# Batch 1's v product behind its scores, x of pair 2 two products behind its v product, and three k transposes moved from TensorE to DMA

## The chip, the cores and the metric

The kernel runs on one core of one Trainium2 chip. The metric is the device time of one execution in microseconds (us), the median of several runs. A ratio in this text is the mean time of one kernel's runs over the mean of the other's runs of the same rounds; it is not quite the ratio of the quoted medians.

Engine names in the profile: PE is TensorE (matrix products), PEld its weight loads, DVE is VectorE, ACT is ScalarE, POOL is GpSimd, SP is SyncE. `banks` is the kernel's name for the buffers in PSUM that TensorE writes. "L583" is line 583 of the kernel's file; the changed kernel has 16 or so more lines, so the same code there has another number.

## The reference

Attention with projected keys and values (Linformer), then a feed-forward layer with a three-way maximum:

```python
batch, n_heads, seq, head_dim = 8, 8, 1024, 64; k_proj = 64
k_proj = einsum('ks,bhsd->bhkd', E, k);  v_proj = einsum('ks,bhsd->bhkd', F, v)
attn   = softmax(q @ k_proj^T / sqrt(64)) @ v_proj
x      = attn.transpose(0, 2, 1, 3).reshape(8192, 512)
out    = maximum(maximum(x @ w1, x @ w2), x @ w3) @ w_out     # d_ff = 768
```

## The kernel before

The feed-forward products of batch b fill TensorE, 512 columns at a time. The attention work of batch b+1 is placed between them, in "visits": a plan says after which step of the feed-forward which piece stands. `(1, 2)` is the visit after step 2 of the second half of the batch; `(1, (3, "mid"))` is inside step 3, after two of its three products of four matmuls. `kproj`, `vproj` are the projections of k and v, `kt` turns the projected k on TensorE, `sc` computes the scores of a pair of heads and their exponentials, `za` the sums and values of a pair (`values` reads the projected v, called vp), `qd` packs q and turns it by DMA into qT, `ld` loads a batch.

```python
    def kt(b):                       # k of batch b turned on TensorE
        def f():
            t, ns = two()
            t = t.bitcast(BF16)[:, 0]
            for gg in range(2):
                nc.tensor.transpose(
                    out=t[:, gg * P:(gg + 1) * P], in_=kps[b][:, gg, :], identity=ident
                )
            pe(0.2)
            kpTs[b] = att.tile([P, NPAIR, KP], BF16, name="kpT")
            copy("v", kpTs[b].rearrange("a (y x) k -> a x y k", x=2),
                 t[:, 0:2 * P].rearrange("a (x y k) -> a x y k", x=2, y=2), ns, 0.3)
        return f

    def plan(b):
        n = b + 1
        if b == 0:
            c1 = (SPC, SPC)
            return {
                ...
                (0, 7): [qd(1, 2), za(0, 2, *c1)],       # q of batch 1 turned, in two DMAs
                (0, 8): [za(0, 3, *c1)],
                (1, 0): [kproj(1)],
                (1, 1): [kt(1)],
                (1, 2): [vproj(1), ld(2)],
                (1, (3, "mid")): [sc(1, 0, now=True), sc(1, 1)],
                (1, 4): [za(1, 0), sc(1, 2, now=True)],
                ...
        # b = 3, 4, 5:
            out[1, 2] = [kproj(n + 1), vproj(n + 1)] + out[1, 2]
            out[1, 3] = [kt(n + 1)]                      # then ld(n + 2)
            out[1, 6] += [sc(n + 1, 0)]
    ...
                up_first({                               # the very first product
                    ...
                    (0, 1, 3): [lambda: v_pair(2), lambda: x(2)],
                    (0, 1, 5): [lambda: v_pair(3), ld(1)],
```

`x(g)` is the values of pair g (which read what `v_pair(g)` and a DVE copy made) and the scaling by the softmax sums. All loads are cast by DMA from GpSimd's queue, in order; SyncE's queue issues qT's transposes, the stores and a few small transfers, also in order.

The softmax here doesn't subtract the row's maximum and nothing guards it: scores larger than these inputs give would overflow.

## Time and profile before

403.06 us (402.93 to 403.52 in 3 runs).

| what | reading | from |
|---|---|---|
| PE busy | 388.4 of 400.4 us | the page, part 1 |
| products of 128x512 | start 216 ns apart | the timeline of PE |
| DMA engines | 9 tenths busy up to 80 us | the page, part 2 |
| longest PE waits after the start | 1.04 us for batch 1's v, 0.45 us for vp of pair 2 | waits and timeline |

Parts 1 and 2 of the page of the kernel before: busy us of each engine with its share of the span, then tenths in 40 slices of 10 us.

```profile
PE 388.4 (97%) x2244; PEld 176.7 (44%) x2286; DVE 203.5 (51%) x319; ACT 151.0 (38%) x242; POOL 34.2 (9%) x49
...
PE   7999989999999999999999999999999999999996
...
PEclk9999999999999999999999999999999999999999
DMA  9999999968799998999989959990890229020202
```

PE is the bound engine nearly everywhere, at its full clock, and DMA is about full through the first eight slices (80 us). PE's busy share alone would not prove that it is at its peak, because pipelined matmuls overlap in the record. The spacing of starts does: 216 ns for 512 columns. The Trainium skill ("TensorE: Matmul & The Clock Gate", section "Wait — 56ns, not 53.3ns?") gives 215.7 ns for warm back-to-back matmuls of that size, and this trace agrees.

The list of waits of PE in the kernel before: who waited for whom, us in total, how often, the longest. A wait of 1.5 us of the warm-up stands above these lines and is left out.

```profile
...
PE banks L346 <- DMA v_t<-in_v_dram: 1.0, 1, 1.0
PE banks L490 <- DMA k_t<-in_k_dram: 0.9, 1, 0.9
PE banks L687 <- issue: 0.8, 5, 0.2
...
PE banks L232 <- DVE vp L102: 0.7, 2, 0.5
PE banks L583 <- DVE xT L309: 0.3, 2, 0.2
PE banks L212 <- DVE m L652: 0.3, 1, 0.3
```

L346 is the projection of k or v, L490 the first k product of batch 0, L232 sums and values, L212 scores, L583 the three up products, L687 the down product. A wait "for issue" here sits where one matmul record is missing from the trace. The line of L346 is the largest wait that a new order of work could take away. The timeline of PE around it, kernel before: start us, duration us, engine, line, what, count, and in brackets the idle time just before and what ended it.

```profile
45.76 2.75 PE L583 MATMUL banks<-xT,w_sb 128*128 128x512 bf16 x12
48.44 1.06 PE L346 MATMUL banks<-k_t,efT 128*64 128x256 bf16 x16
...
52.04 0.27 PE L432 MATMUL banks<-ident,kp 128*128 128x128 bf16 x2
52.15 2.75 PE L583 MATMUL banks<-xT,w_sb 128*128 128x512 bf16 x12
55.95 1.06 PE L346 MATMUL banks<-v_t,efT 128*64 128x256 bf16 x16 [1.04 <-DMA v_t<-in_v_dram]
56.94 1.90 PE L583 MATMUL banks<-xT,w_sb 128*128 128x512 bf16 x8
58.77 0.63 PE L212 MATMUL banks<-qT,kpT 64*64 64x512 bf16 x8
59.33 1.04 PE L583 MATMUL banks<-xT,w_sb 128*128 128x512 bf16 x3
```

The v product starts at 55.95, the moment its load has landed (issued at 25.64, landed at 55.90), and the scores follow at 58.77. The scores read qT. The trace's record of the issue of qT's first half, at 43.95 us in the kernel before, says when it landed:

```profile
DMA to landing us min/median/max: 13.2/13.2/13.2
```

That is at 57.16, so at 58.77 nobody waits for it.

The timeline of PE around pair 2's values (L232 at 21.25), kernel before:

```profile
19.31 1.04 PE L583 MATMUL banks<-xT,w_sb 128*128 128x512 bf16 x4
20.19 0.61 PE L516 MATMUL banks<-v_t,efT 128*128 128x128 bf16 x8
21.25 0.30 PE L232 MATMUL banks<-pT,vp 64*64 64x256 bf16 x4 [0.45 <-DVE vp L102]
21.48 0.60 PE L583 MATMUL banks<-xT,w_sb 128*128 128x512 bf16 x2
```

And around the turn of batch 5's k (L432):

```profile
206.82 0.28 PE L432 MATMUL banks<-ident,kp 128*128 128x128 bf16 x2
206.93 1.24 PE L583 MATMUL banks<-xT,w_sb 128*128 128x512 bf16 x5
```

The record of the two transposes lasts 0.28 us, but the next product starts 0.11 us after the first of them: that, and not the duration, is what they cost a pipelined PE.

### The profile page before, as it was taken

To read this page: it belongs to the slowest core of one execution; us is meant where nothing else is said; L and a number is where in the kernel's file an instruction comes from. 1 tells how busy PE (TensorE), PEld (TensorE's weight loads), DVE (VectorE), ACT (ScalarE), POOL (GpSimd) and SP (SyncE) were. 2 spreads that over 40 slices of the span, in tenths; PEclk is the share of its full clock that TensorE was granted. 3 is DMA by queue.
4 is the path that set the end of the run, shared out by engine and by line. 5 is a ranking of instruction groups with operands and counts; after the bars stand their busy time and mean duration, and the time that the engine had idled before them with its cause. 6 is when DMAs were issued, how large, how long until landed. Compare 5 with 4: busy or idle time off the path is not lost.

```text
span 400.4 us, 5708 instructions
## 1 busy us (share of the span) xinstructions
PE 388.4 (97%) x2244; PEld 176.7 (44%) x2286; DVE 203.5 (51%) x319; ACT 151.0 (38%) x242; POOL 34.2 (9%) x49
## 2 busy tenths in 40 slices
PE   7999989999999999999999999999999999999996
PEld 3444443353444445444454445444454444444443
DVE  2348746762683525736274544744267342745251
ACT  2535428527222462253323532245323533132312
POOL 7440002000400200010020000100000000000000
PEclk9999999999999999999999999999999999999999
DMA  9999999968799998999989959990890229020202
GB/s 159 205 206 208 230 204 156 235 137 156 203 187 198 221 218 193 223 183 209 224 221 178 236 133 269 178 242 26 204 217 5 103 67 252 0 105 2 105 0 105
DMA packets 66330, 66.09 MB, mean 165 GB/s; under 512 B 30624, under 2 KB 58784, under 8 KB 66304
## 3 DMA queue, kind: packets, MB, share of 16 engines
q0 software_dynamic: 29104, 30.41, 47.0%
q1 hardware_dynamic: 37056, 35.20, 34.3%
q8 instruction: 17, 0.28, 0.3%
q10 hardware_dynamic: 144, 0.13, 0.1%
q14 instruction: 9, 0.07, 0.1%
HBM read 69.73 MB, written 16.97 MB: 217 GB/s over the span
## 4 chain that ended last, share of the span: by engine, by line
PE 84%; DMA 9%; DVE 2%; issue 2%; ACT 1%; POOL 0%; DVEq 0%; ACTq 0%; POOLq 0%
PE banks L583 56%; PE banks L687 18%; DMA v_t<-in_v_dram 8%; PE banks L346 3%; PE banks L232 2%; PE banks L212 2%; DMA k_t<-in_k_dram 2%; DVE xT L309 1%; PE banks L257 1%; ACT zi_all L298 1%; ACT zl L292 1%; PE banks L490 1%; DVE m L652 0%; PE banks L461 0%; PE banks L516 0%
## 5 line engine op out<-in xcount | busy, mean ns | idle before, releaser
L583 PE MATMUL banks<-xT,w_sb 128*128 128x512 bf16 x1119 | 254.8, 379 | 2.6 <-issue 0.8
L583 PEld LDWEIGHTS <-w_sb 128*128 128x128 bf16 x1152 | 109.9, 98 | 136.1 <-issue 8.5
L652 DVE TENSOR_TENSOR m<-banks,h1s 128x512 f32<-128x512 f32 x90 | 62.1, 690 | 135.3 <-ACT h1s L648 92.7
L648 ACT COPY h1s<-banks 128x512 f32<-128x512 f32 x90 | 52.6, 585 | 120.3 <-PE banks L583 118.8
L687 PE MATMUL banks<-wout_sb,hT 128*128 128x512 bf16 x370 | 85.6, 379 | 1.0 <-issue 0.8
L593 DVE TENSOR_TENSOR hT<-banks,m 128x512 bf16<-128x512 f32 x90 | 62.3, 692 | 9.3
L687 PEld LDWEIGHTS <-hT 128*128 128x128 bf16 x378 | 35.2, 98 | 47.4 <-issue 5.6
L102 ACT COPY o_sb<-banks 128x512 f32<-128x512 f32 (+1 forms) x56 | 32.6, 582 | 57.9 <-PE banks L687 57.6
L223 ACT ACTIVATE pT<-banks 128x1024 bf16<-128x1024 f32 (+1 forms) x36 | 32.8, 932 | 18.1 <-PE banks L212 18.1
L309 DVE TENSOR_TENSOR xT<-banks,zi_all 128x1024 bf16<-128x1024 f32 x28 | 33.1, 1219 | 11.7 <-PE banks L232 6.9
L201 POOL DMA_DIRECT2D q_t<-in_q_dram x7 | 6.1, 878 | 193.8 <-DMA qT<-q_p 118.8
L346 PEld LDWEIGHTS <-efT 128*64 128x64 bf16 x224 | 11.6, 110 | 4.5 <-issue 3.0
L102 DVE CAST vp<-banks 64x256 bf16<-64x256 f32 (+1 forms) x18 | 7.1, 397 | 12.5 <-ACT vp L102 9.5
L102 ACT CAST vp<-banks 64x256 bf16<-64x256 f32 x14 | 5.1, 364 | 21.4 <-PE banks L346 21.3
L232 PE MATMUL banks<-pT,vp 64*64 64x512 bf16 (+1 forms) x144 | 11.4, 364 | 0.7 <-DVE vp L102 0.7
L212 PE MATMUL banks<-qT,kpT 64*64 64x512 bf16 (+1 forms) x144 | 11.4, 362 | 0.4 <-DVE m L652 0.3
L292 ACT ACTIVATE zl<-banks 128x512 f32<-128x512 f32 (+1 forms) x12 | 8.9, 739 | 6.3 <-PE banks L232 5.3
L102 DVE COPY q_p<-q_t 128x1024 bf16<-128x1024 bf16 x28 | 10.4, 435 | 0.5 <-DMA q_t<-in_q_dram 0.5
L346 PE MATMUL banks<-v_t,efT 128*64 128x256 bf16 x112 | 7.3, 273 | 1.0 <-DMA v_t<-in_v_dram 1.0
L102 DVE COPY o_sb<-banks 128x512 f32<-128x512 f32 (+1 forms) x9 | 5.8, 653 | 4.5 <-PE banks L667 4.5
L346 PE MATMUL banks<-k_t,efT 128*64 128x256 bf16 x112 | 7.4, 276 | 0.0
L461 PE MATMUL banks<-warm_f 128*128 128x512 f32 x8 | 6.0, 895 | 1.5 <-DVE warm_f L175 1.5
(63 smaller groups left out, 120.9 us busy)
## 6 DMA issues: line engine op xcount, KB each, us to landing
out_dram<-o_sb SPq DMA_DIRECT2D x30, 512.0 KB, 4.6
zi_all<-zd SPq DMA_DIRECT2D x20, 512.0 KB, 8.0
q_t<-in_q_dram POOLq DMA_DIRECT2D x7, 1024.0 KB, 10.1
k_t<-in_k_dram POOLq DMA_DIRECT2D x7, 1024.0 KB, 16.4
v_t<-in_v_dram POOLq DMA_DIRECT2D x7, 1024.0 KB, 21.9
zi_all<-zd POOLq DMA_DIRECT2D x4, 512.0 KB, 7.6
w_sb<-in_moe_w_dram POOLq DMA_DIRECT2D x4, 384.0 KB, 11.1
k_t<-in_k_dram POOLq DMA_DIRECT2D x2, 512.0 KB, 8.7
```

The lines of the kernel that those rows point to most:

```text
L102: done = {"v": nc.vector.tensor_copy, "s": nc.scalar.copy, "g": nc.gpsimd.tensor_copy}[eng](out=o, in_=i)
L212: nc.tensor.matmul(out=t[c * HALF:(c + 1) * HALF, hp, 0:n * P], lhsT=kpTs[b][rows, g, :], rhs=qTs[b][rows, at:at + n, :], start=True, stop ...
L223: nc.scalar.activation(out=pTs[b, g, lo], in_=t, func=AF.Exp, scale=scale)
L232: nc.tensor.matmul(out=t[hp * HALF:(hp + 1) * HALF, c, 0:nsi * HALF], lhsT=w(rows, hp), rhs=p[rows, hp, :], start=True, stop=True,)
L292: nc.scalar.activation(out=zl, in_=t, func=AF.Ln)
L309: nc.vector.tensor_tensor(out=xTs[b][:, g, lo:lo + nsi, :].rearrange("a (c s) p -> a c (s p)", c=2), in0=t, in1=zi, op=ALU.mult,)
L346: nc.tensor.matmul(out=t[hh * HALF:(hh + 1) * HALF, 0:width], lhsT=efT[:, si, (kv - 1) * KP:kv * KP], rhs=qkv[b][kv][:, heads[hh], si, :], ...
L583: nc.tensor.matmul(out=h, lhsT=w_sb[i][:, ct, jt * P:(jt + 1) * P], rhs=xTs[b][:, ct, ch * SPC:(ch + 1) * SPC, :], start=(ct == first), st ...
L593: nc.vector.tensor_tensor(out=o, in0=h, in1=other, op=ALU.max)
L648: nc.scalar.copy(out=h1s, in_=h[0][0])
L652: nc.vector.tensor_tensor(out=m12, in0=h[1][0], in1=h1s, op=ALU.max)
L687: nc.tensor.matmul(out=o_ps, lhsT=hTs[b, ch][:, jt, tt * P:(tt + 1) * P], rhs=wout_sb[:, jt, :], start=(jt == 0), stop=(jt == NJT - 1),)
```

## The change

Three parts. A: batch 1's v product goes behind its scores, so that it does not wait for its load, and its k product and turn go one step later. B: pair 2's v product goes two products earlier, so that the copy of vp runs behind products. C: k of batches 5 to 7 is turned by a DMA on SyncE's queue instead of TensorE and a DVE copy; the next batch's loads wait for that DMA.

```diff
+            if i == 0 and b - 1 in turned:          # in load(): q waits for the turned k
+                after(dma, turned[b - 1])
+    def k_pair(b, g):
+        if b in turned:
+            return kpTs[b][:, g % 2, (g // 2) * KP:(g // 2 + 1) * KP]
+        return kpTs[b][:, g, :]
 ...
-                    lhsT=kpTs[b][rows, g, :],
+                    lhsT=k_pair(b, g)[rows],
 ...
+    def kd(b):
+        def f():
+            kpTs[b] = att.tile([P, 2, 2 * KP], BF16, name="kpT2")
+            turned[b] = nc.sync.dma_start_transpose(
+                out=kpTs[b], in_=kps[b].rearrange("a g x -> a (g x)")
+            )
+        return f
 ...
-                (1, 0): [kproj(1)],
-                (1, 1): [kt(1)],
-                (1, 2): [vproj(1), ld(2)],
-                (1, (3, "mid")): [sc(1, 0, now=True), sc(1, 1)],
+                (1, 1): [kproj(1)],
+                (1, 2): [kt(1)],
+                (1, (3, "mid")): [sc(1, 0, now=True), sc(1, 1), vproj(1), ld(2)],
 ...
-            out[1, 2] = [kproj(n + 1), vproj(n + 1)] + out[1, 2]
-            out[1, 3] = [kt(n + 1)]
+            out[1, 2] = [kproj(n + 1), kd(n + 1), vproj(n + 1)] + out[1, 2]
 ...
-                    (0, 1, 3): [lambda: v_pair(2), lambda: x(2)],
+                    (0, 1, 1): [lambda: v_pair(2)],
+                    (0, 1, 3): [lambda: x(2)],
```

More of the change, by code (lines that the diff above doesn't have):

```diff
@@ L203, in load @@
                 after(dma, last_T[b - 1])
+            if i == 0 and b - 1 in turned:
[4 more added lines that the diff above has]
+        return kpTs[b][:, g, :]
+    turned = {}
     def scores(b, g, lo, nsi):
@@ L758, in plan @@
             out[0, 4] = [qd(n + 1)]
-            out[1, 2] = [kproj(n + 1), vproj(n + 1)] + out[1, 2]
-            out[1, 3] = [kt(n + 1)]
+            out[1, 2] = [kproj(n + 1), kd(n + 1), vproj(n + 1)] + out[1, 2]
             out[1, 6] += [sc(n + 1, 0)]
         if n + 2 < B:
-            out[1, 3] += [ld(n + 2)]
+            out[1, 3] = [ld(n + 2)]
         return out
```

## The prediction

> **What bounds the kernel now.** TensorE. The busy table gives PE 388.4 of 400.4 us. In the timeline 128x512 products start 216 ns apart almost everywhere, at a granted clock of 1.0; the Trainium skill ("TensorE: Matmul & The Clock Gate", section "Wait — 56ns, not 53.3ns?") gives 215.7 ns for warm back-to-back matmuls, and the trace agrees. From batch 2 on the list of waits has no PE wait on another engine of 0.1 us or more. So idle time can be won only before about 77 us; elsewhere only PE work removed counts.
>
> **The change, costed.**
>
> A. Batch 1, 48 to 60 us. The list of waits has one PE wait of 1.04 us for batch 1's v, which lands at 55.90 (timeline: v product at 55.95). After, the v product (0.99 us) stands behind the scores, so v is there. But the scores come early: from 45.76 to 58.77 is 13.0 us; without the v product (1.1 with its switch) and the wait (1.1) they are due at about 56.5. They read qT of pairs 0 and 1, whose DMA transpose was issued at 43.95 and landed at 57.16. The DMA engines are 9 tenths busy up to there, so this landing should not move. I expect a new PE wait of about 0.7 us on qT before batch 1's first scores. One switch between products (0.09 us) goes. Gain about 0.45 us, not 1.1.
>
> B. Pair 2. Before, the values waited 0.45 us for the copy of vp (v product at 20.19, copy 20.90 to 21.20, values 21.25). The v product now stands two products (0.43 us) earlier, but its slice of v landed only at 20.05. It starts at about 20.1 after waiting 0.3 us, and the values still come 1.06 us later, near 21.15. Gain about 0.1 us, and the wait for qT in A, bound by DMA, swallows most of it.
>
> C. k of batches 5 to 7 turned by DMA. Removes six PE transposes, 0.055 us each start to start: 0.11 us per batch, 0.33 us in all, on the saturated PE; also three DVE copies of 0.28 us, off the path. (The skill, same page, "Part 4: PE-mode transpose", says about 275 ns each in a kernel; this trace shows 55.) The DMA transposes are two blocks each against qT's 32; behind two output stores they should land 3 to 6 us after the k product, and their scores come about 11 us after it. The next loads wait for that landing, 1 to 4 us, with over 15 us to spare. No new PE wait.
>
> D. The bank hand-out shifts. The v copies (ACT 0.74, DVE 0.87 us) run between exponentials near 59 us, ready before the values at 62.5. The 0.27 us bank wait near 67.6 stays. Worth -0.2 to +0.3 us.
>
> **Sum.** About 0.5 + 0.33 = 0.85 us, all on the critical path: 402.2 us, 0.2% faster. 8 in 10: 401.4 to 402.9. Chances: faster by over 2% 0.01, within 2% 0.98, slower 0.01.
>
> **What would show it.** List of waits: v_t wait of 1.04 gone, a PE wait of 0.5 to 1.0 us on the qT transpose at about 57 us; near 20 us a PE wait for v_t of about 0.3. Batch 1's first output products (68.2 before) 0.5 us earlier. PE shorter by 0.11 at each old transpose of batches 5 to 7; kpT's DMA landing before its scores.
>
> **What would make it wrong.** qT landing earlier (A and B together up to 1.4 us); bank waits of the new order at 59 to 68 us; the small DMA transposes landing over 10 us late, which would stall PE three times; run noise of 0.3 us.

## The result, and the profile after

402.0 us (401.62 to 402.24 in 4 runs) against 403.0 us (402.42 to 403.52 in 4 runs); ratio 0.9975, 95% interval 0.9958 to 0.9992. The output is correct.

The list of waits of PE in the changed kernel (L221 is the scores, L533 pair 2's v product, L241 sums and values), again without the warm-up's 1.5 us:

```profile
...
PE banks L221 <- DMA qT<-q_p: 1.0, 1, 1.0
PE banks L507 <- DMA k_t<-in_k_dram: 0.8, 1, 0.8
...
PE banks L533 <- DMA v_t<-in_v_dram: 0.3, 1, 0.3
PE banks L221 <- DVE m L669: 0.3, 1, 0.3
...
PE banks L241 <- DVE vp L102: 0.2, 1, 0.2
```

The wait of 1.0 us for batch 1's v is gone, and one of 1.0 us for qT stands in its place. (New too: 0.7 us for the identity matrix. It ends at 6.48 us, in the warm-up, ahead of the wait for the first k; two other traces of the same kernel don't list it.) The timeline of PE of the changed kernel there:

```profile
50.97 1.06 PE L355 MATMUL banks<-k_t,efT 128*64 128x256 bf16 x16
51.97 2.76 PE L600 MATMUL banks<-xT,w_sb 128*128 128x512 bf16 x12
54.57 0.28 PE L441 MATMUL banks<-ident,kp 128*128 128x128 bf16 x2
54.68 1.89 PE L600 MATMUL banks<-xT,w_sb 128*128 128x512 bf16 x8
57.58 0.63 PE L221 MATMUL banks<-qT,kpT 64*64 64x512 bf16 x8 [1.01 <-DMA qT<-q_p]
58.13 1.06 PE L355 MATMUL banks<-v_t,efT 128*64 128x256 bf16 x16
59.13 1.04 PE L600 MATMUL banks<-xT,w_sb 128*128 128x512 bf16 x3
```

The scores now come early and wait until 57.58 for qT. The record of the issue of qT's first half (43.90 us) in the changed kernel:

```profile
DMA to landing us min/median/max: 13.6/13.6/13.6
```

It landed at 57.54. When step 3's third product goes on, at 59.13, the same work is done as at 59.33 before. That is a gain of only 0.20 us, in a run whose loads came 0.4 us later (v landed at 56.32, not 55.90). The same work counted from v's landing ends after 3.43 us before (59.33 - 55.90) and after 2.81 us now (59.13 - 56.32): part A is worth 0.62 us on equal loads. The later loads are not the change's doing as far as the record shows: the runs of B alone and C alone, which leave batch 1's order as it was, have v at 56.69 and 56.35.

Around pair 2's values, changed kernel:

```profile
19.23 0.60 PE L600 MATMUL banks<-xT,w_sb 128*128 128x512 bf16 x2
20.12 0.62 PE L533 MATMUL banks<-v_t,efT 128*128 128x128 bf16 x8 [0.28 <-DMA v_t<-in_v_dram]
20.57 0.59 PE L600 MATMUL banks<-xT,w_sb 128*128 128x512 bf16 x2
21.19 0.30 PE L241 MATMUL banks<-pT,vp 64*64 64x256 bf16 x4
```

The v product was called earlier, waited for its slice of v and started at 20.12 instead of 20.19; the values came at 21.19 instead of 21.25. The products before it were already 0.08 us earlier (19.23 against 19.31), so nothing was won.

Where batch 5's k was turned, the timeline of PE shows 18 products without a break:

```profile
204.19 4.05 PE L600 MATMUL banks<-xT,w_sb 128*128 128x512 bf16 x18 [0.16 <-issue]
```

The last PE instruction ends at 396.53 instead of 397.11, 0.58 us earlier: 0.20 of that is won by 68 us (the down product starts at 67.99 instead of 68.19), and most of the rest at the three removed turns.

### The profile page after: what moved, and what is told of

It is laid out like the page before. It is cut to its first block, busy times and chain, and to the rows that moved or that the text cites. A ratio compares the mean times of both kernels' runs of the same rounds, so it can differ in the third digit from the quotient of the medians.

```text
span 400.1 us, 5695 instructions
## 1 busy us (share of the span) xinstructions
PE 387.7 (97%) x2238; PEld 176.3 (44%) x2280; DVE 203.0 (51%) x316; ACT 151.1 (38%) x242; POOL 34.3 (9%) x49
## 4 chain that ended last, share of the span: by engine, by line
PE 86%; DMA 7%; DVE 2%; ACT 2%; issue 2%; POOL 1%; DVEq 0%; ACTq 0%; POOLq 0%
PE banks L600 58%; PE banks L704 19%; DMA qT<-q_p 3%; DMA v_t<-in_v_dram 3%; PE banks L355 3%; PE banks L241 2%; PE banks L221 2%; PE banks L266 1%; DVE xT L318 1%; ACT zl L301 1%; ACT zi_all L307 1%; DVE m L669 0%; POOL k_t L152 0%; POOL q_t L157 0%; POOL v_t L152 0%
## 5 line engine op out<-in xcount | busy, mean ns | idle before, releaser
L669 DVE TENSOR_TENSOR m<-banks,h1s 128x512 f32<-128x512 f32 x90 | 62.1, 690 | 132.8 <-ACT h1s L665 90.4
L221 PE MATMUL banks<-qT,kpT 64*64 64x512 bf16 (+1 forms) x144 | 11.4, 361 | 1.4 <-DMA qT<-q_p 1.0
L241 PE MATMUL banks<-pT,vp 64*64 64x512 bf16 (+1 forms) x144 | 11.4, 364 | 0.3 <-DVE vp L102 0.2
L221 PEld LDWEIGHTS <-kpT 64*64 64x64 bf16 x144 | 4.0, 105 | 8.0 <-issue 5.6
```

What stands on the lines that cost most here:

```text
L221: nc.tensor.matmul(out=t[c * HALF:(c + 1) * HALF, hp, 0:n * P], lhsT=k_pair(b, g)[rows], rhs=qTs[b][rows, at:at + n, :], start=True, stop= ...
L241: nc.tensor.matmul(out=t[hp * HALF:(hp + 1) * HALF, c, 0:nsi * HALF], lhsT=w(rows, hp), rhs=p[rows, hp, :], start=True, stop=True,)
L669: nc.vector.tensor_tensor(out=m12, in0=h[1][0], in1=h1s, op=ALU.max)
```

## The experiments

Twelve runs were made on the chip, all with a correct result; all timed runs were of the fast state, and the single run without rounds is of unknown state. For each profiled run I read three things from the trace: the largest PE waits, the landing of batch 1's v, and the end of the last PE instruction. The difference of the last two takes the scatter of the start and of the loads out of the comparison, as long as PE stands waiting for DMA at about 57 us. There is only one trace of the kernel before.

| run | time, us | ratio to before (95%) | v landed | last PE end | difference |
|---|---|---|---|---|---|
| before | 403.06 | | 55.90 | 397.11 | 341.21 |
| after | 402.0 | 0.9975 (0.9958 to 0.9992) | 56.32 | 396.53 | 340.21 |
| after_again | 402.21 | 0.9981 (0.9959 to 1.0002) | 56.01 | 396.18 | 340.17 |
| after_third | 402.01 | 0.9987 (0.9976 to 0.9999) | 56.31 | 396.47 | 340.16 |
| a_only | 402.03 | 0.9976 (0.9956 to 0.9996) | 56.20 | 396.83 | 340.63 |
| b_only | 402.95 | 0.9997 (0.9977 to 1.0016) | 56.69 | 398.47 | 341.78 |
| c_only | 402.82 | 0.9993 (0.9974 to 1.0013) | 56.35 | 397.20 | 340.85 |
| k_old_slot | 402.64 | 0.9990 (0.9969 to 1.0012) | 56.40 | 397.90 | 341.50 |
| k4_dma | 403.51 | 1.0012 (0.9984 to 1.0040) | 56.56 | 397.92 | 341.36 |
| v_first | 401.39 | 0.9958 (0.9942 to 0.9974) | 57.40 | 397.05 | 339.65 |
| v_first_again | 401.4 | 0.9970 (0.9958 to 0.9983) | 56.34 | 395.70 | (339.36) |
| v_first_x_late | 401.77 | 0.9968 (0.9951 to 0.9985) | 56.41 | 395.86 | (339.45) |
| stores_late | 400.92 | 0.9961 (0.9949 to 0.9973) | 55.30 | 395.55 | (340.25) |
| v_held | 407.79 (one run) | none | 62.48 | 402.36 | (339.88) |

The differences in brackets are not compared. In v_first_again, v_first_x_late and stores_late PE doesn't wait at 57 us at all, so that its own lateness is still in them (it comes 0.36, 0.45 and 1.25 us after v's landing); in v_held a load is held on purpose.

My theory (theory 1): batch 1's scores and values are paced by two DMA landings, v and then qT about 1.2 us later, and not by PE's order. The change swaps a wait for the first against a wait for the second, part B falls in front of those landings and is swallowed, and part C takes 0.33 us of real PE work away. Rivals: the gain comes from A alone and C is free or harmful; or the wait for v was won whole; or something unseen in one trace adds 0.4 us.

Two readings of the traces need no common start at all, and separate A from C better than any timing here:

- *What paces batch 1.* With the old order (before, b_only, c_only) step 3's third product starts 3.43 us after v has landed, in all three. With A's order (the changed kernel three times, a_only, k_old_slot, k4_dma) it starts 1.59 or 1.60 us after qT has landed, in all six. So A is worth 1.83 us less the time between the two landings: 0.62, 0.68 and 0.67 us in the three traces of the changed kernel, and a loss of 0.66 us in k_old_slot, where qT landed 2.50 us after v.
- *What the turns cost.* From the k product of batch 5, 6 or 7 to the first scores of that batch it is 12.16 us in every trace that turns k on PE (before, a_only, b_only) and 12.05 us in all eleven that turn it by DMA. That is 0.11 us for each turn, 0.33 us in all.

### The changed kernel again

No edit.

> The changed kernel once more, timed in more rounds, because the first timing (0.9975 of before, 0.9958 to 0.9992) does not tell 0.6 us from 1.5 us. Theory 1 (what the traces show: one PE wait traded for another, and six transposes gone): 0.6 us less than before, ratio about 0.9985. Rival (something the single trace does not show, worth another 0.4 us): 1.0 us less, ratio about 0.9975. In the trace: a PE wait on qT of 0.7 to 1.1 us near 57 us again, none on v_t there.

Ratio 0.9981. PE waited 0.90 us for qT near 57 us. The ratio lies between the two expected ones and its interval covers both. The differences 340.21, 340.17 and 340.16 of the three traces do agree within 0.05 us, and lie 1.00 to 1.05 us under before. So theory 1's 0.6 us, read from the start of a single trace, was itself too small: in the first trace v landed 0.42 us later than in the trace of before, which hid that much of a gain of 1.0 us. Nothing unseen is needed.

### Part A alone

Edit: only the four plan lines of batch 1.

> Only the move of batch 1's k and v products. Theory 1 (the wait moves from v to qT): 0.1 to 0.4 us less than before, PE wait on qT of 0.5 to 1.1 us near 57 us. Rival (the move wins the whole v wait, and the k part wins nothing): 1.0 us less than before, no PE wait over 0.3 us there.

Ratio 0.9976; difference 340.63, 0.58 us under before. The PE wait for qT was only 0.25 us in this trace, because its start was late: the first k product began at 10.36 us (9.59 in the changed kernel).

```profile
57.53 0.63 PE L212 MATMUL banks<-qT,kpT 64*64 64x512 bf16 x8 [0.25 <-DMA qT<-q_p]
```

Still the scores started at 57.53, against 57.58. PE came there 0.7 us later and lost nothing, which is what a wait for a DMA landing does. Both signs went the rival's way, a wait under 0.3 us and about 1.0 us by the timing (interval 0.2 to 1.8); theory 1's 0.1 to 0.4 us was too small. What speaks against the rival is the trace: the wait was short because PE came late, and counted from v's landing A won 0.58 us (0.55 us up to step 3's third product), not 1.0.

### Part B alone

Edit: only the two lines of `v_pair(2)` and `x(2)`.

> Only pair 2's v product and x apart by two products. Theory 1: within 0.15 us of before. PE waits near 20 us: about 0.3 us for v_t and under 0.1 us for vp, where before had 0.45 us for vp; and the 1.0 us wait for batch 1's v at 56 us grows by what is won, since its landing is bound by DMA. Rival (two products hide the copy): 0.4 us less than before.

Ratio 0.9997. PE waited 0.39 us for pair 2's v instead of 0.45 us for its copy, and 1.31 us for batch 1's v. Its difference, 341.78, contains one wait of 0.42 us at 170 us for the qT of batch 4, which other traces mostly lack; the excess over before, 0.57 us, lies all between the k products of batch 4 and batch 5, where that wait stands. Before it nothing differs: from v's landing to the first down product both kernels take 12.29 us. So what B did ahead of v's landing was worth nothing behind it. The rival's 0.4 us would need the slice of v (which landed at 20.05 in the trace of before) to be there earlier.

### Part C alone

Edit: the change without its plan lines for batch 1 and pair 2.

> Only k of batches 5 to 7 by DMA. Theory 1: 0.33 us less than before (3 x 0.11 us of PE), no new PE wait, and the DMA transposes land at least 4 us before the scores that read them. Rival (transposes on a pipelined PE cost nothing, or the DMA disturbs): 0 to 0.2 us more than before.

Ratio 0.9993: 0.28 us less, not told from zero by the timing. The difference is 340.85, 0.36 us under before, and no new PE wait appears. By the timings alone A could be the whole gain; that C has its part is shown by the stretches of 12.16 and 12.05 us above. Together A and C make 0.94 us of the changed kernel's 1.00 to 1.05. The DMA transposes landed at 209.70, 253.82 and 299.90, 4.6 to 7.2 us before their scores.

### The k product in its old slot

```diff
-                (1, 1): [kproj(1)],
-                (1, 2): [kt(1)],
+                (1, 0): [kproj(1)],
+                (1, 1): [kt(1)],
```

> The changed kernel with batch 1's k product and its turn in their old slots; only the v product is moved. Theory 1 (qT's landing bounds the visit): same time as the changed kernel within 0.2 us, the same PE wait on qT of about 1.0 us. Rival (the later k product is part of the gain): 0.3 us or more slower than the changed kernel, with a PE wait for k_t or kp before it.

Ratio 0.9990, inconclusive. The timeline of PE in this run:

```profile
50.01 1.06 PE L355 MATMUL banks<-k_t,efT 128*64 128x256 bf16 x16 [1.33 <-DMA k_t<-in_k_dram]
...
58.94 0.63 PE L221 MATMUL banks<-qT,kpT 64*64 64x512 bf16 x8 [0.74 <-DMA qT<-q_p]
```

In its trace the load of k landed at 49.97 (47.76 in the trace of before, 49.04 after), so the k product in the old slot waited 1.33 us for it, as the rival said; but then the scores waited another 0.74 us for qT, which landed at 58.90 in this run. The loss for k was paid before another wait and was not the bound: the last PE instruction ends 339.00 us after qT's landing, as in the changed kernel (338.99 to 339.01). Whether qT's late landing had to do with the order or was a slow run of the loads is open. What this run does show is that the later slot takes the k product out of reach of a late load.

### The load of v held

```diff
+            if i == 2 and b == 1:                   # in load(): v waits for qT's first half
+                after(dma, half_T[0])
 ...
-                    (0, 1, 5): [lambda: v_pair(3), ld(1)],
+                    (0, 1, 5): [lambda: v_pair(3), ld(1, (0, 1))],
 ...
-                (0, 7): [qd(1, 2), za(0, 2, *c1)],
+                (0, 7): [qd(1, 2), za(0, 2, *c1), ld(1, (2,))],
```

> The changed kernel with the load of batch 1's v held until the first half of its qT has landed: less DMA traffic next to that transpose. A diagnosis, not an improvement. Theory 1 (qT lands late because loads share the DMA engines): the first half of qT lands under 9 us after its issue instead of 13.6, before 53 us; the PE wait on qT at 57 us is gone, and PE waits 2 to 6 us for v instead. Rival (the transpose takes 13 us by itself): it lands at 57 us as before.

The record of the issue of qT's first half (44.01 us) in this run:

```profile
DMA to landing us min/median/max: 8.4/8.4/8.4
```

It landed at 52.41, five microseconds earlier, with v's load out of its way. So qT is late because it shares the DMA engines with loads, and the rival (13 us by itself) falls. The load of v itself, issued at 52.96 here, landed 9.5 us later, where in the changed kernel it takes 30.6 us. The timeline of PE in this run:

```profile
56.62 0.63 PE L224 MATMUL banks<-qT,kpT 64*64 64x512 bf16 x8
62.52 1.92 PE L358 MATMUL banks<-v_t,efT 128*64 128x256 bf16 x16 [5.28 <-DMA v_t<-in_v_dram]
```

The window of 62.1 to 65.5 us of the same run (length, busy us and instructions of PE, PEld, DVE, ACT, POOL, then the granted clock, DMA share and GB/s):

```profile
62.10:65.50 3.40, 2.76 (x18) 1.89 (x19) 0.25 (x1) 0.99 (x3) 0.76 (x1) 0.51 1.14 184
```

The scores did not wait; the v product waited 5.28 us. After that idle time the granted clock was 0.51 for 3.4 us, and the v product took 1.92 us instead of 1.06. The Trainium skill ("TensorE: Matmul & The Clock Gate", section "HAM oscillation — how this bites in real kernels") has the rule of no PE idle gaps over about 3.4 us; this run agrees with its one gap of 5.28 us, and the waits of about 1 us in the kernels before and after cost no clock (1.00 from 54 to 60 us). Where between the two the limit lies, no run here shows.

### The v product ahead of the scores in the same visit

The two waits of the traces suggest a better order. PE comes to the visit at about 56.6 us, when v has landed and qT has about 1 us to go, and the v product takes 1.0 us.

```diff
-                (1, (3, "mid")): [sc(1, 0, now=True), sc(1, 1), vproj(1), ld(2)],
+                (1, (3, "mid")): [vproj(1), sc(1, 0, now=True), sc(1, 1), ld(2)],
```

> The changed kernel with batch 1's v product ahead of the scores in the same visit. PE reaches that visit at about 56.6 us; v landed at 55.9 to 56.3, qT at 57.2 to 57.5, and the v product takes 1.0 us, so it fills the wait for qT. Theory 1 (both landings are set by DMA, not by PE's order): no PE wait over 0.3 us between 45 and 65 us, 0.8 to 1.0 us less than the changed kernel, 1.4 to 1.7 us less than before. Rival (later stages are bound by ACT's exponentials or by banks, so that the wait comes back): waits of 0.5 us or more between 59 and 77 us, and under 0.4 us less than the changed kernel.

> The changed kernel with batch 1's v product ahead of the scores, again. Theory 1: 0.9 us less than the changed kernel where v lands before PE comes for it, 0.5 us less where PE waits for v; ratio to before about 0.9957. Last PE instruction 339.2 to 339.7 us after the landing of v. Rival (the gain of the first timing was the noise of the start): ratio to before 0.9975 or more.

> The changed kernel, for a comparison on one chip with the two runs after it. About 0.9975 of before: 0.93 us less when the landing of batch 1's v is the same. In the trace the last PE instruction ends about 340.2 us after that landing (before: 341.2).

Ratios 0.9958 and 0.9970. On one chip, in the same rounds, the changed kernel had 402.01 us (0.9987) and this one 401.4 us (0.9970), and the means differ by 0.74 us. Both ratios missed what was expected (0.9975 and 0.9957), by about 0.5 us each: the kernel before ran faster in these rounds (mean 402.62 us) than in the others (402.96 to 403.07), and the second interval still reaches the rival's 0.9975. It is the comparison of the two in the same rounds that shows the gain. The timeline of PE of the second run, where v had landed in time:

```profile
56.70 1.06 PE L355 MATMUL banks<-v_t,efT 128*64 128x256 bf16 x16
57.70 0.63 PE L221 MATMUL banks<-qT,kpT 64*64 64x512 bf16 x8
58.26 1.04 PE L600 MATMUL banks<-xT,w_sb 128*128 128x512 bf16 x3
59.51 2.76 PE L600 MATMUL banks<-xT,w_sb 128*128 128x512 bf16 x12 [0.22 <-DVE vp L102]
```

Both waits are gone: v landed at 56.34, qT at 57.51, and the v product fills the time between. A new wait of 0.22 us for the copies of vp appears at 59.51. Step 3's third product starts 1.92 us after v's landing (58.26 - 56.34), against 2.81 us in the changed kernel, although PE came 0.36 us after that landing. In the first run, v landed late (57.40) and PE waited 0.64 us for it, against the expectation of no wait over 0.3 us; that run also had a wait of 0.42 us for batch 4's qT, and still stood 0.5 us under the changed kernel's difference. The rival about later stages is not borne out: the only new wait between 59 and 77 us is that of 0.2 us.

### Pair 2's x two products later instead

```diff
-                    (0, 1, 1): [lambda: v_pair(2)],
-                    (0, 1, 3): [lambda: x(2)],
+                    (0, 1, 3): [lambda: v_pair(2)],
+                    (0, 0, 5): [lambda: x(2)],
```

on top of the v product ahead of the scores.

> As the run with the v product ahead of the scores, and pair 2's v product back in its old place with x two products behind it. Theory 1: the PE waits near 20 us (v_t 0.28, vp 0.02) are gone, PE comes to batch 1 some 0.3 us earlier and waits there up to 0.2 us for v_t, which lands when DMA lets it: 0.1 to 0.3 us less than that run. Rival (the early saving is kept in full): 0.35 us less.

Ratio 0.9968 against 0.9958, not told apart; the differences can't decide it either, since PE waits for no landing in them. The waits for v and vp near 20 us are gone, but a wait of 0.33 us for DVE's x appeared at 22.73: pair 3's v product now waits for the scaling of pair 2, most likely for the bank that it reads. Theory 1's 0.1 to 0.3 us is not seen, and the rival's 0.35 us neither.

### The store behind qT

On top of the v product ahead of the scores, the first store of batch 0 (512 KB, issued at 43.2 just ahead of qT's transposes) is issued after both of them:

```diff
+    held = []
 ...
         elif tt % 2:
-            nc.sync.dma_start(out=ov[:, si - 1:si + 1, :], in_=o_sb)
+            held.append((ov[:, si - 1:si + 1, :], o_sb))
+            if (b, ch, tt) != (0, 0, 1):
+                for o, i in held:
+                    nc.sync.dma_start(out=o, in_=i)
+                held.clear()
```

> As v ahead of the scores, and the first output store of batch 0 (issued at 43.3, just ahead of batch 1's qT transpose) issued after both of its halves. Theory 1 (DMA sharing sets these landings): qT's first half lands 1 to 3 us earlier after its issue than 13.6 us, v some 1 us earlier; no PE wait on v or qT at 56 to 58 us; 0 to 0.6 us less than the run with v ahead, never more than 0.2 us slower. Rival (the store does not matter to them): landings as before, same time.

The record of qT's first half (43.95 us):

```profile
DMA to landing us min/median/max: 12.5/12.5/12.5
```

It landed at 56.47, and v at 55.30, each about 1 us earlier than in v_first_again. This is one trace, but both are the earliest of all traces in which v's load was not held (v 55.90 to 57.40, qT 57.16 to 58.90). PE waited for neither. Ratio 0.9961, 400.92 us, against 401.4 us on the same chip without this edit; the intervals overlap, so of the two it can only be said that this one is no slower. It is the lowest median of all kernels here, and its whole interval (0.9949 to 0.9973) lies below that of the changed kernel in the same rounds (0.9976 to 0.9999).

### k of batch 4 by DMA too

```diff
-                (1, 3): [kproj(4), vproj(4), ld(5), vx(3, 0), vx(3, 1)],
-                (1, 4): [kt(4)],
+                (1, 3): [kproj(4), kd(4), vproj(4), ld(5), vx(3, 0), vx(3, 1)],
```

> The changed kernel with k of batch 4 turned by DMA too. Theory 1 (SyncE issues in order, and the issue of batch 4's qT transpose holds it from 154 to 167 us): k's transpose is issued at about 167 us and lands after 169, where its scores stand at 168.7 us: a PE wait of 1 to 3 us on it, and 1 to 2.5 us slower than the changed kernel. Rival (the small transpose passes): another 0.1 us less than the changed kernel.

Ratio 1.0012, 0.3% above the ratios of the changed kernel, which were measured in other rounds. The timeline of SyncE's queue in this run (start, time that the issue took):

```profile
154.13 12.06 SPq L421 DMA_TRANSPOSE qT<-q_p  x1
166.29 0.53 SPq L718 DMA_DIRECT2D out_dram<-o_sb  x1
166.91 1.37 SPq L456 DMA_TRANSPOSE kpT<-kp  x1
```

And the timeline of PE at the scores of batch 4:

```profile
169.86 0.41 PE L221 MATMUL banks<-qT,kpT 64*64 64x512 bf16 x4 [1.35 <-DMA kpT<-kp]
```

Issuing qT's transpose holds SyncE for 12.06 us, so the small one, whose input was ready at 158.94, could be issued at 166.91 only, landed at 169.81, and the scores waited 1.35 us for it. That is why the DMA turn starts with batch 5: there the queue is free at 203 us, 10 us before the scores.

## Why the prediction was right or wrong, point by point

The predicted 402.2 us (401.4 to 402.9) stands against 402.0 us; the three ratios of the changed kernel average 0.9981, about 0.77 us of 403, and the traces give 1.0 us on equal loads, where 0.85 was predicted. That 402.2 and 402.0 lie so close is partly luck: the interval of the first ratio allows a gain of 0.3 to 1.7 us. Point by point:

- A, the exchange of a wait for v against a wait for qT: right. Predicted 0.7 us of new wait, measured 1.01, 0.90 and 0.78 us in three traces. The gain, put at 0.45 us, measured 0.62 us on equal loads and 0.58 us alone. The term that was off is the new wait, put at about 0.7 us: PE takes 10.87 us from the start of its step to the scores (45.70 to 56.57 after), so on the times of the trace before it would come at 56.63 and wait 0.57 us until 57.20. The estimate also let part B bring PE there about 0.1 us earlier, which B did not do.
- A, that qT's landing does not move: about right, 57.16 before and 57.17 to 57.54 in the three traces of the changed kernel. That it is sharing which makes it late was only argued from the DMA share in the prediction; the run with v held shows it (8.4 us instead of 13.6).
- B, about 0.1 us and mostly swallowed: the wait of 0.3 us for the slice of v came as predicted (0.28). What was won is nearer to zero than to 0.1 us.
- C, 0.11 us for each of three turns: right, 12.16 us against 12.05 us at each of them in every trace, and 0.36 us in all by the trace of C alone. The landing was put at 3 to 6 us after the k product. It came 6.7 us after its end at batch 5 (202.44 to 209.16) and earlier later on. The scores read it at 213.59, so this cost nothing. The loads of batches 6 and 7 were issued 2.6 and 4.7 us later than before (207.52 to 210.14, 249.40 to 254.05), not 1 to 4; the last v of them landed at 277.25, 18 us before its use.
- D, the bank wait near 67.6 us stays: it did, 0.27 us both times.
- The first down product of batch 1 was to come 0.5 us earlier and came 0.20 us earlier in the profiled run, because that run's loads were 0.4 us later. A single trace against a single trace hides a gain of this size when the stretch is paced by DMA.

## What to carry to other kernels

When the wait on a load is taken away by moving its reader, look up when the other inputs of the visit land before counting the gain: here the next landing was 1.2 us behind, so that of a wait of 1.04 us about 0.6 us was won, and the product that had been moved away was just the work to fill that time. Work saved ahead of such a landing was worth nothing here (part B), while work taken off the saturated engine behind it was kept in full (part C). To judge half a microsecond, count from the landing that paces the stretch and not from the start of the trace.

## What the Trainium skill lacked or had wrong

- "TensorE: Matmul & The Clock Gate", section "Part 4: PE-mode transpose", puts a 128x128 bf16 transpose at about 275 ns in a kernel. That is a duration, and here the record lasts 219 ns; what the section lacks is the spacing, which is what a busy PE pays: 55 ns from start to start among other products, and removing six saved 0.33 us. The same page's 55.6 ns between warm matmuls of 128 columns fits that. So the 275 and the 55 ns that the prediction sets side by side are not the same quantity.
- "Advanced Engine Details and Errata", section "X-Bar Transpose (TRN2)", says that transpose DMAs are as fast as regular ones. No run here compares the two, so none shows it wrong. What the section lacks is how much other transfers delay one: beside the loads, half of qT (512 KB) took 12.5 to 14.8 us to land; with one load of 1 MB held back, 8.4 us.
- I found no page that gives, for Trainium2 by name, the time for which issuing a DMA transpose holds SyncE's queue against later issues: 10.8 to 12.4 us for the 32-block transposes of qT of batches 4 to 7 in the trace of before, 1.2 to 2.2 us for the two blocks of k in the changed kernel. It is no fixed cost: the same 32 blocks took 4.9 us at batch 2 and 19.9 us at batch 3.
